# A gated mix of an S5 scan and an H3 convolution: the first time block's two pairs of B.x are turned by ScalarE, and halves, gates and scalings change places

## The chip, the core and the metric

The kernel runs on one core of one Trainium2 chip. The core has TensorE (PE, matmuls), VectorE (DVE), ScalarE (ACT), GpSimd (POOL) and SyncE (SP); each takes its own instructions in order, and they wait for one another by semaphores. DMAs are issued here from SyncE's queue (plain and transposing loads, stores) and from GpSimd's (gathers that add to what lies at their destination); a few small loads come from ScalarE's. The metric is the time of one execution on the device, in microseconds, as the median of several runs. The profile's trace is that of a single execution.

## The reference, cut to what matters

Inputs are bf16; x is [1, 2048, 1024] (time by channel), and the state has P = 1024 complex components.

```python
def _A_ref(x, Lambda_re, Lambda_im, B_re, B_im, C_re, C_im, log_dt, Dskip):
    Lam_bar = jnp.exp(jnp.exp(log_dt) * Lam)
    B_bar = ((Lam_bar - 1.0) / Lam)[:, None] * Bmat
    Bu = jnp.einsum("bld,pd->blp", x + 0j, B_bar)
    for t in range(L):
        h = Lam_bar[None, :] * h + Bu[:, t, :]
    y = 2.0 * jnp.einsum("blp,dp->bld", hseq, Cmat).real + x * Dskip
def _B_ref(q, k, v, shift_k, ssm_k, ssm_D):
    kv = k_shift * v            # k_shift: 4 taps of k along time
    y = irfft(rfft(kv_pad) * rfft(kf_pad))[:S] + kv * ssm_D
    return q * y
g = sigmoid((x * gate_w).sum(-1, keepdims=True))
out = g * _A_ref(x, ...) + (1 - g) * _B_ref(x, B_k, B_v, ...)
```

## The kernel before, in words

**Two halves.** The H3 part (the long convolution `_B_ref`) goes channel tile by channel tile, eight tiles of 128 channels; its results go to a scratch tensor in DRAM (`cv_scr`). The S5 part (`_A_ref`) goes by time blocks of 512 steps (`tb` 0 to 3) and by groups of 256 state components (`g` 0 to 3). It starts as filler between the H3 rounds and then has the rest of the kernel.

**A round of the H3 part** is one pass of the loop `for c in range(NC - 1)` (L1132), c = 0 to 6; the eighth channel's products follow behind the loop. Round c does the products in frequency of channel c on VectorE (`products`, L664), the transform of the next channel n = c + 1 on TensorE (`fwd_K`, `fwd_V`, into PSUM tiles `psk` and `psv`, which ScalarE evicts to Kh and Vh), the inverse transform of channel c - 1 (`inverse`, L716, PSUM tile `psz`, evicted to `cv` and stored), and the taps of channel c + 2 (`taps`, L562). `times_v` (L592) multiplies the tap sums `ks` by v on VectorE and then mirrors them on TensorE. The first product of a channel, `G<-Kh,Vh` (or `G<-BT,Vh`, where an even channel's spectrum of K lies in a tile named BT), reads the whole of Vh. A second part of G is added by a gather from GpSimd (`G<-wkh`).

**B.x** is computed for 16 blocks (`order`, L766): the list index i runs over (tb, g) = (0,0), (0,1), (1,0), (1,1), (2,0) and so on. A block has two tiles (j = 0, 1) of 128 components. The time steps of a block are kept as evens (a = 0) and odds (a = 1), 256 each, since the scan runs over pairs of steps: an even step's entry is turned into even + lam times the odd step before it. x is loaded transposed, in two halves: half h of time block tb holds the steps of parity h (`load_xT`, L250), and a = h reads it. Block 1's half 1 is loaded in round 2 and its half 0 in round 3, at L1228:

```python
            if nn + 1 < NC:
                load("kT", nn + 1, True)
                load("kn", nn + 1)
                apart = spread(nn + 1)
                step(apart)
...
                elif c in (2, 3):
                    load_xT(1, (3 - c,))
```

`load(..., True)` writes a column with ScalarE first (`hold`), so that the load waits for ScalarE's place in the order. `spread` copies kT to kB on SyncE's queue.

**The lam-multiples** are made in two ways. Blocks i = 0 and 1 (time block 0) use `Bu_tile` (L813): TensorE multiplies the odd steps by diagonal matrices of lam (`lamd`, made by `lam_diag`, L770: four times 128x128 products with the identity and two with -lam's for each group, by ScalarE in round 0 and by VectorE in round 1) and adds them in PSUM. All other blocks use `turn_U` (L872): six ScalarE passes write lam times the odd steps to a tile Q, in two parts, and after each part a gather from GpSimd adds Q to the evens. Blocks 2 and 3 are computed by `Bu_halves` (L838), odds first, then evens, each 16 matmuls of 256 columns; from block 4 on by `Bu_plain` (512 columns).

**The order.** Every engine's instructions stand in the order of the program (`put`, L92). The tiles of blocks 0 to 3 are one generator, `parts` (L1129), and each `step(parts)` in a round takes it to its next `yield`. A tile of `Bu_tile` has three steps (odds, evens, lam matmuls), and a tile of `Bu_halves` also has three (odds, evens, nothing). The 24 calls: round 1 four (before the taps, after `times_v`, two between the halves of `fwd_V`), round 2 five, round 3 four, round 4 five, round 5 four, round 6 two.

**After the rounds.** `gate(tb)` (L748) are 32 matmuls of one column and two small sigmoids. C's eight tiles (`turn_C`, L1274) are scaled too: m = the other part times a factor (ScalarE), the tile times its factor (ScalarE for tiles 0 and 1, VectorE for the others), and then the sum, for tiles 0, 1, 4, 5 by gathers. Tiles 4 and 5 keep m in the four buffers of the pool Q, where `turn_U` of the later blocks gets its Q as well. The 16 scans (`scan`, L891) then run on VectorE, each with 256-long scans, rotations, and lam-multiples q of the result hb, by VectorE or, for the scans in `scaled_by_act`, by ScalarE. TensorE multiplies by C (`Cy`, `Cy_group`, PSUM tile `psy`). Filler steps that a loop puts on the list `on_act` are taken between B.x tiles (`Bu_next`, L1365). `stamp` (L1169) is a small GpSimd copy at the start of round 6 that waits for x of time block 2.

Of the kernel before, what the change touches and what calls it, by code (L numbers as in the profile page):

```python
# [20 lines left out]
def kernel(  # L21
# [64 lines left out]
    def ps2(shape, name):  # L86
        return psum.tile(shape, F32, name=name, tag="ps")
# [29 lines left out]
    def act(o, i, **kw):  # L117
        put("act", nc.scalar.activation, out=o, in_=i, **kw)
# [648 lines left out]
    order += [(NTB - 1, g) for g in range(NG)]  # L767
    ends = consts.tile([128, 2, NG, 2, 2], BF16, name="ends")

    def lam_diag(g, home, on_act=False):  # L770

        if g == 0:
            lamd["all"] = home.tile([128, 2, 2, 3, 128], BF16, name="lamd", tag="lamd")
        t = lamd[g] = lamd["all"][:, g]
        for j in range(2):
            for k, f in enumerate((lam[:, 0], lam[:, 1], mlam)):
                pi = 2 * g + j
                if on_act:
                    act(t[:, j, k], ident, func=ACT.Identity, scale=f[:, pi:pi + 1])
                else:  # L780
                    ts(t[:, j, k], ident, f[:, pi:pi + 1], None, ALU.mult)

    def Bu(i):
        tb, g = order[i]
        if i == 13:
            V_ = s5p["v13"].tile([128, 2, 2, HB], BF16, name="V13")
            O_ = lam_pool.tile([128, 2, 2, HB + 2], BF16, name="O13", tag="lamd")
            Us[tb, g] = V_, O_[:, :, :, 2:]
            turns_U[i] = turn_U(g, V_, O_)
            return [Bu_plain(tb, g, V_, O_, j) for j in range(2)]  # L790
        if i in (10, 11):
            if i == 10:
                s5p["u2"] = xt_pool.tile([128, 2, 2 * (4 * HB + 4)], BF16, name="U2", tag="xT")
            U = s5p["u2"][:, i - 10]
        else:
            shape = [128, 2 * (4 * HB + 4)]
            if i in (6, 7, 8, 15):
                U = u4(shape, BF16, "U")
            else:
                home = uu[0 if i in (0, 1, 14) else 1] if i < 6 or i == 14 else s5p["uu"]  # L800
                U = home.tile(shape, BF16, name="U")
        if i >= 2:
            V_, O_ = U[:, 0:4 * HB], U[:, 4 * HB:]
            V_ = V_.rearrange("p (c j t) -> p c j t", c=2, j=2)
            O_ = O_.rearrange("p (c j t) -> p c j t", c=2, j=2)
            Us[tb, g] = V_, O_[:, :, :, 2:]
            turns_U[i] = turn_U(g, V_, O_)
            return [(Bu_halves if i < 4 else Bu_plain)(tb, g, V_, O_, j) for j in range(2)]
        U = U[:, 0:8 * HB].rearrange("p (a c j t) -> p a c j t", a=2, c=2, j=2)
        Us[tb, g] = U[:, 0], U[:, 1]  # L810
        return [Bu_tile(tb, g, U, j) for j in range(2)]

    def Bu_tile(tb, g, U, j):  # L813
        xT = xTs[tb]
        ps = []
        d = lamd[g][:, j]
        for a in (1, 0):
            ps.append(ps2([128, 2, HB], ("even", "odd")[a]))
            for c in range(2):
                for dt_ in range(ND):  # L820
                    mm(ps[1 - a][:, c], BT[g][:, c, dt_, j * 128:(j + 1) * 128], xT[:, dt_, a * HB:(a + 1) * HB],
                       dt_ == 0 and (a == 1 or c == 0), a == 1 and dt_ == ND - 1)
            if a == 1:
                act(U[:, 1, :, j], ps[0], func=ACT.Copy)
                if j == 1 and tb < NTB - 1:
                    act(ends[:, tb % 2, g], U[:, 1, :, :, HB - 1], func=ACT.Copy)
                yield
        yield
        for k, c, o in ((0, 0, 0), (0, 1, 1), (1, 0, 1), (2, 1, 0)):
            if tb > 0:  # L830
                mm(ps[1][:, o, 0:1], d[:, k], ends[:, 1 - tb % 2, g, c, j:j + 1], False, False)
            mm(ps[1][:, o, 1:HB], d[:, k], U[:, 1, c, j, 0:HB - 1], False, k == 2)
        act(U[:, 0, :, j], ps[1], func=ACT.Copy)
        yield

    turns_U = {}

    def Bu_halves(tb, g, V_, O_, j):  # L838
        if j == 0:
            act(O_[:, :, :, 1], ends[:, 1 - tb % 2, g], func=ACT.Copy)  # L840
        for a in (1, 0):
            ps = ps2([128, 2, HB], ("even", "odd")[a])
            for c in range(2):
                for dt_ in range(ND):
                    mm(ps[:, c], BT[g][:, c, dt_, j * 128:(j + 1) * 128], xTs[tb][:, dt_, a * HB:(a + 1) * HB],
                       dt_ == 0, dt_ == ND - 1)
# [7 lines left out]
        yield  # L854

    def Bu_plain(tb, g, V_, O_, j):
        xT = xTs[tb]
        if j == 0 and tb > 0:
            act(O_[:, :, :, 1], ends[:, 1 - tb % 2, g], func=ACT.Copy)
        elif j == 0:  # L860
            act(O_[:, :, :, 1], lam[:, :, 0:2], func=ACT.Copy, scale=0.0)
        ps = ps2([128, 2, 2, HB], "both")
        for c in range(2):
            for dt_ in range(ND):
                mm(flat(ps[:, c]), BT[g][:, c, dt_, j * 128:(j + 1) * 128], xT[:, dt_], dt_ == 0, dt_ == ND - 1)
        act(O_[:, :, j, 2:], ps[:, :, 1], func=ACT.Copy)
        if j == 1 and tb < NTB - 1:
            act(ends[:, tb % 2, g], O_[:, :, :, HB + 1], func=ACT.Copy)
        act(V_[:, :, j], ps[:, :, 0], func=ACT.Copy)
        yield  # L870

    def turn_U(g, V_, O_):  # L872
        both = slice(0, 2)
        for part in (((both, both, lam[:, 0]),), ((0, 1, lam[:, 1]), (1, 0, mlam))):
            if s5p["Q"] is s5p["wu"]:
                if part[0][0] == both:
                    whole_Q = u4([128, 2, 2, 2, HB], BF16, "Q")
                Q = whole_Q[:, part[0][0] != both]
            else:
                Q = s5p["Q"].tile([128, 2, 2, HB], BF16, name="Q")  # L880
            for j in range(2):
                pi = 2 * g + j
                for c, o, f in part:
                    act(Q[:, o, j], O_[:, c, j, 1:1 + HB], func=ACT.Identity, scale=f[:, pi:pi + 1])
            gather(V_, Q)
            yield

    put_off = []
    scaled_by_act = (4, 12, 13, 14)

    def scan(tb, g, fin):  # L891

# [6 lines left out]
        for js in ([slice(0, 1), slice(1, 2)] if last else [slice(0, 2)]):  # L899
# [39 lines left out]
            if tb * NG + g == 3:  # L939
                run(turning[7])  # L940
                product(0)
            if by_act and tb == NTB - 1:
                q = [s5p["Q"].tile([128, 2, 2, HB], BF16, name="Q") for k in range(2)]
            else:
                q = [w2([128, 2, 2, HB], BF16, "q") for k in range(2)]
# [119 lines left out]
    def step(gen):  # L1065
        next(gen, None)
# [65 lines left out]
    for c in range(NC - 1):  # L1132
        n, nn = c + 1, c + 2
        if c == 0:
# [28 lines left out]
            step(apart)  # L1163
            load_xT(0, (1,))
            run(apart)
            lam_diag(0, lam_pool, True)
            continue
        if c == 6:
            put("pool", nc.gpsimd.tensor_copy, stamp, xTs[2][:, 0, 0:HB + 1:HB])  # L1169
# [1 line left out]
        step(old)  # L1171
        step(tabs)
        if c == 6:
            step(parts)
        step(back)
        step(tv)
        steps(prod, 3)
# [11 lines left out]
        if c == 2:  # L1189
            step(parts)  # L1190
        fwd_K(n, (0, 1))
        if c in (2, 6):
            step(parts)
        fwd_K(n, (2, 3))
        if c == 4:
            step(parts)
# [6 lines left out]
        if nn < NC:  # L1203
# [2 lines left out]
            step(fk)  # L1206
            if c < 5:
                step(fk)
            if c == 4:
                step(parts)  # L1210
            if c == 1:
                load_BT(1, 0, True)
            elif c < 5:
# [35 lines left out]
            run(next(tiles))  # L1249
            run(next(tiles))  # L1250
        fwd_V(n, (0, 1))
        if c < 6 and c != 4:
            step(parts)
            if c in (1, 3):
                step(parts)
        fwd_V(n, (2, 3))
        if c in (4, 5):
            step(parts)
        if c == 1:
            lam_diag(1, lam_pool)  # L1260
        old = tabs

    h3r.close()
# [10 lines left out]
    def turn_C(pi):  # L1274
# [7 lines left out]
            act(m[c], CT[pi][:, 1 - c], func=ACT.Identity, scale=mc2i[:, pi:pi + 1])  # L1282
            yield
        for c, f in enumerate((c2r, mc2r)):
            if pi < 2:
                act(CT[pi][:, c], CT[pi][:, c], func=ACT.Identity, scale=f[:, pi:pi + 1])
            else:
                ts(CT[pi][:, c], CT[pi][:, c], f[:, pi:pi + 1], None, ALU.mult)
            if by_sum:
                gather(CT[pi][:, c], m[c])  # L1290
        if not by_sum:
            tt(CT[pi], CT[pi], whole_m, ALU.add)

# [4 lines left out]
    with tc.tile_pool(name="fin", bufs=1, side="right") as fin:  # L1298
# [6 lines left out]
        prod, back = products(c, 0, room, False), inverse(c - 1)  # L1305
        run(old)
        steps(prod, 3)
        run(turns_U[3])
        run(next(tiles))
        steps(turning[0], 2)  # L1310
        step(back)
        steps(turning[1], 2)
        run(back)
        gate(1)
        gate(2)
        steps(prod, 2)
        b6, b7 = Bu(6)
        run(b6)
        run(b7)
        run(turns_U[6])  # L1320
        run(turning[0])
# [111 lines left out]
    for j in range(NS):  # L1433
# [6 lines left out]
        advance(j)  # L1440
        for t in turning[2 * j:2 * j + 2]:
            run(t)
        on_act += [lambda t=t: step(t) for t in turning[2 * j + 2:2 * j + 4] for _ in range(2)]
        turn = turns_U[turned[j]] if j in turned else none
        if j != 10 and plan[j][0:1] != "G":
            step(turn)
# [82 lines left out]
```

## Time and profile before

| what | value |
| --- | --- |
| median of 3 runs | 384.33 us (384.24 to 385.03) |
| the profiled execution | 384.57 us, span of its instructions 382.8 us |
| granted TensorE clock, mean | 0.998 |
| ScalarE's passes of one turn (171.20 to 174.0 us) | 2.85 us |
| matmul of 512 / 256 columns, start to start | 0.216 / 0.11 us |
| DMA | 71.77 MB, mean 187 GB/s |
| gather U<-Q, 256 KB, issue to landing, median | 5.3 us |
| gather G<-wkh, 768 KB, issue to landing, median | 8.8 us |

How to read it: times within the trace are microseconds from the first instruction of the program. The listing by groups gives out<-in by the program's names, so `even<-U,lamd` is a matmul that writes the PSUM tile "even" from U and lamd; nearly all instructions stand at L94, the helper that issues them, so tiles tell more than lines. A timeline row is start, duration, engine, line, operation, out<-in, shape and count, and in brackets how long the engine was idle before it and what ended that. Matmuls overlap in the pipeline, so the distance between starts tells more of their rate than their duration does.

### The profile page before, as it was taken

The page shows a single profiled execution, that of the slowest core. Times are in us where ns is not written, and L with a number is a line of the kernel's source. Part 1 is how long each engine was busy: PE and PEld are TensorE (multiplying, and loading weights), DVE is VectorE, ACT ScalarE, POOL GpSimd, SP SyncE. Part 2 cuts the span into 40 slices and gives each one's busy share as a digit, 9 for nine tenths or more (in the row PEclk, how much of TensorE's full clock was granted, in tenths as well). Part 3 has the DMA queues.
Part 4 walks back from the last instruction along what each step waited for, and adds up shares of the span by engine and source line. Part 5 has one row for each costly group of instructions (what it writes and reads, how often), then busy time and mean ns, then how long its engine had stood idle before and what let it go on. Part 6 is the DMA issues. An engine that isn't in the chain of part 4 may idle for free.

```text
span 382.8 us, 6633 instructions
## 1 busy us (share of the span) xinstructions
PE 371.3 (97%) x2419; PEld 198.3 (52%) x2453; DVE 371.2 (97%) x599; ACT 303.6 (79%) x469; POOL 81.8 (21%) x108
## 2 busy tenths in 40 slices
PE   7899999999999999999999999989999999999995
PEld 5566458575584846744454444434444444444442
DVE  7999999999999999999999999999999999999996
ACT  5898998988979999786979699675989759937601
POOL 4011030020301102031003110413414323634100
PEclk9999999999999999999999999999999999999999
DMA  7979999998999997959999999986899999898903
GB/s 166 165 108 223 218 205 205 245 203 211 201 164 211 208 213 169 198 125 154 192 221 164 226 203 250 213 153 125 150 222 192 208 245 246 136 250 156 238 8 110
DMA packets 126402, 71.77 MB, mean 187 GB/s; under 512 B 104665, under 2 KB 107489, under 8 KB 126370
## 3 DMA queue, kind: packets, MB, share of 16 engines
q1 hardware_dynamic: 111232, 45.64, 55.4%
q0 software_dynamic: 12976, 25.17, 38.9%
q10 hardware_dynamic: 2162, 0.54, 0.8%
q8 instruction: 19, 0.31, 0.3%
q14 instruction: 13, 0.11, 0.1%
HBM read 15.48 MB, written 8.39 MB: 62 GB/s over the span
## 4 chain that ended last, share of the span: by engine, by line
PE 52%; DVE 30%; issue 9%; DMA 4%; ACT 3%; ACTq 1%; POOL 0%; DVEq 0%; POOLq 0%
PE psy L94 29%; PE both L94 15%; DVE BT L94 11%; DVE wkh L94 8%; DVE G L94 5%; DVE t L94 3%; PE psz L94 2%; DVE ks L94 2%; PE psk L94 2%; DMA CT<-Q 2%; DMA pbb<-cv_scr 1%; PE psv L94 1%; DMA rows<-in_gate_w_dram 1%; PE p L94 1%; PE taps L94 1%
## 5 line engine op out<-in xcount | busy, mean ns | idle before, releaser
L94 PEld LDWEIGHTS <-BT 128*128 128x128 bf16 x640 | 62.0, 98 | 48.3 <-issue 0.2
L94 PE MATMUL both<-xT,BT 128*128 128x512 bf16 x375 | 83.0, 379 | 0.4
L94 POOL DMA_DIRECT2D U<-Q x26 | 26.7, 1039 | 88.8 <-ACT Q L94 31.0
L94 PEld LDWEIGHTS <-hb 128*128 128x128 bf16 x256 | 24.9, 98 | 31.4 <-issue 1.6
L94 PEld LDWEIGHTS <-U 128*128 128x128 bf16 x240 | 23.5, 98 | 28.3
L94 PE MATMUL psy<-CT,hb 128*128 128x512 bf16 x157 | 36.3, 379 | 0.1
L94 ACT ACTIVATE Vh<-psv 128x1024 bf16<-128x1024 f32 x32 | 30.7, 1034 | 5.3 <-PE psv L94 5.3
L94 PE MATMUL psy<-CT,U 128*128 128x512 bf16 x149 | 34.6, 379 | 0.2
L94 ACT ACTIVATE Q<-U,lam 128x512 bf16<-128x512 bf16 (+1 forms) x52 | 29.9, 612 | 4.9 <-DMA CT<-Q 4.9
L94 DVE TENSOR_TENSOR_SCAN W<-rv,init,A 128x256 bf16<-128x256 f32 x48 | 32.2, 730 | 0.0
L94 POOL DMA_DIRECT2D G<-wkh x8 | 9.7, 1218 | 102.8 <-DVE wkh L94 102.8
L94 ACT ACTIVATE U<-both 128x512 bf16<-128x512 f32 x44 | 24.1, 595 | 8.0 <-PE both L94 7.5
L94 PEld LDWEIGHTS <-SF 128*128 128x128 bf16 x184 | 18.0, 98 | 19.7 <-issue 1.4
L94 PE MATMUL psk<-eok,SF 128*128 128x512 bf16 (+1 forms) x119 | 27.9, 354 | 0.3
L94 PE MATMUL psz<-G,CI 128*128 128x512 bf16 x64 | 24.3, 379 | 0.1
L94 PE MATMUL psz<-G,SI 128*128 128x512 bf16 x64 | 24.3, 379 | 0.0
L94 PE MATMUL psy<-CTa,hb 128*128 128x512 bf16 x94 | 22.6, 379 | 1.2 <-ACT U L94 1.0
L94 PE MATMUL taps<-dg,kT 128*128 128x128 bf16 (+1 forms) x352 | 21.7, 210 | 0.8 <-DMA kT<-in_B_k_dram 0.8
L94 PEld LDWEIGHTS <-kT 128*128 128x128 bf16 x352 | 21.0, 100 | 2.5 <-DMA kT<-in_B_k_dram 2.1
L94 DVE TENSOR_TENSOR wkh<-BT,Vh 128x3072 bf16<-128x3072 bf16 (+4 forms) x20 | 21.8, 1110 | 0.0
L94 DVE TENSOR_TENSOR wkh<-Kh,Vh 128x3072 bf16<-128x3072 bf16 (+2 forms) x16 | 21.2, 1348 | 0.0
L94 PE MATMUL psy<-CTa,U 128*128 128x512 bf16 x87 | 20.4, 379 | 0.1
(227 smaller groups left out, 846.1 us busy)
## 6 DMA issues: line engine op xcount, KB each, us to landing
U<-Q POOLq DMA_DIRECT2D x26, 256.0 KB, 5.3
G<-wkh POOLq DMA_DIRECT2D x6, 768.0 KB, 8.8
cv_scr<-cv SPq DMA_DIRECT2D x16, 256.0 KB, 5.7
kn<-in_B_ssm_k_dram SPq DMA_DIRECT2D x5, 512.0 KB, 4.0
v<-in_B_v_dram SPq DMA_DIRECT2D x5, 512.0 KB, 6.2
out_dram<-m SPq DMA_DIRECT2D x8, 256.0 KB, 4.5
BT<-cv_scr SPq DMA_DIRECT2D x7, 256.0 KB, 5.9
out_dram<-BT SPq DMA_DIRECT2D x7, 256.0 KB, 2.0
```

The source lines that it names most:

```text
L94: i = f(*a, **kw)
```

## The change

Blocks 0 and 1 are computed by `Bu_halves` too and turned by ScalarE and gathers; `Bu_tile` and `lam_diag` go. A tile now has two steps, so 16 calls of `step(parts)` are left: three in round 1, four in round 2, three each in rounds 3, 4 and 5, none in round 6. The turn of block 0 stands at the start of round 6, that of block 1 where block 3's stood, and block 3's turn goes behind the first tile of block 6; where `s5p["Q"]` is None, their Q lies in the table NCF and in the room of `lamd`. Gates 1 and 2 move ahead of the inverse transform of channel 6. C's tiles 4 and 5 are scaled by ScalarE, with their gathers inside the filler steps. Scan 11's lam-multiples go to ScalarE, with q in the pool Q.

```diff
-    def lam_diag(g, home, on_act=False):
...
     def Bu(i):
...
-        if i >= 2:
-            V_, O_ = U[:, 0:4 * HB], U[:, 4 * HB:]
...
-        return [Bu_tile(tb, g, U, j) for j in range(2)]
-
-    def Bu_tile(tb, g, U, j):
...
+        V_, O_ = U[:, 0:4 * HB], U[:, 4 * HB:]
+        V_ = V_.rearrange("p (c j t) -> p c j t", c=2, j=2)
+        O_ = O_.rearrange("p (c j t) -> p c j t", c=2, j=2)
+        Us[tb, g] = V_, O_[:, :, :, 2:]
+        turns_U[i] = turn_U(g, V_, O_)
+        return [(Bu_halves if i < 4 else Bu_plain)(tb, g, V_, O_, j) for j in range(2)]
     def Bu_halves(tb, g, V_, O_, j):
         if j == 0:
-            act(O_[:, :, :, 1], ends[:, 1 - tb % 2, g], func=ACT.Copy)
+            before(tb, g, O_)
...
             yield
-        yield
+
+    def before(tb, g, O_):
+        if tb > 0:
+            act(O_[:, :, :, 1], ends[:, 1 - tb % 2, g], func=ACT.Copy)
+        else:
+            act(O_[:, :, :, 1], lam[:, :, 0:2], func=ACT.Copy, scale=0.0)
...
+            elif s5p["Q"] is None and part[0][0] == both:
+                Q = NCF.rearrange("p o (j t) -> p o j t", j=2)
+            elif s5p["Q"] is None:
+                Q = lam_pool.tile([128, 2, 2, HB], BF16, name="Qb", tag="lamd")
...
-    scaled_by_act = (4, 12, 13, 14)
+    scaled_by_act = (4, 11, 12, 13, 14)
...
-            if by_act and tb == NTB - 1:
+            if by_act and tb > 1:
...
-            lam_diag(0, lam_pool, True)
...
         if c == 6:
-            step(parts)
+            s5p["Q"] = None
+            run(turns_U[0])
...
         fwd_K(n, (0, 1))
-        if c in (2, 6):
-            step(parts)
         fwd_K(n, (2, 3))
...
-            if c == 4:
-                step(parts)
...
         fwd_V(n, (0, 1))
-        if c < 6 and c != 4:
+        if c < 4:
             step(parts)
-            if c in (1, 3):
-                step(parts)
         fwd_V(n, (2, 3))
-        if c in (4, 5):
+        if c == 5:
             step(parts)
-        if c == 1:
-            lam_diag(1, lam_pool)
...
-            if pi < 2:
+            if by_sum:
                 act(CT[pi][:, c], CT[pi][:, c], func=ACT.Identity, scale=f[:, pi:pi + 1])
             else:
                 ts(CT[pi][:, c], CT[pi][:, c], f[:, pi:pi + 1], None, ALU.mult)
             if by_sum:
                 gather(CT[pi][:, c], m[c])
+                yield
...
-        run(turns_U[3])
+        run(turns_U[1])
         run(next(tiles))
+        gate(1)
+        gate(2)
         steps(turning[0], 2)
         step(back)
         steps(turning[1], 2)
         run(back)
-        gate(1)
-        gate(2)
         steps(prod, 2)
         b6, b7 = Bu(6)
         run(b6)
+        s5p["Q"] = None
+        run(turns_U[3])
+        s5p["Q"] = s5p["wu"]
         run(b7)
...
-        on_act += [lambda t=t: step(t) for t in turning[2 * j + 2:2 * j + 4] for _ in range(2)]
+        if j > 0:
+            on_act += [lambda t=t: step(t) for t in turning[2 * j + 2:2 * j + 4] for _ in range(4 if j == 1 else 2)]
```

More of the change, by code (lines that the diff above doesn't have):

```diff
@@ L768 @@
     ends = consts.tile([128, 2, NG, 2, 2], BF16, name="ends")
-    def lam_diag(g, home, on_act=False):
[L772 to L781, printed above, removed]
     def Bu(i):
@@ L801, in Bu @@
                 U = home.tile(shape, BF16, name="U")
-        if i >= 2:
-            V_, O_ = U[:, 0:4 * HB], U[:, 4 * HB:]
[L804 to L810, printed above, removed]
-        return [Bu_tile(tb, g, U, j) for j in range(2)]
-    def Bu_tile(tb, g, U, j):
[L814 to L826, printed above, removed]
-                yield
[L828 to L834, printed above, removed]
+        V_, O_ = U[:, 0:4 * HB], U[:, 4 * HB:]
[4 more added lines that the diff above has]
+        return [(Bu_halves if i < 4 else Bu_plain)(tb, g, V_, O_, j) for j in range(2)]
     turns_U = {}
@@ L853, in Bu_halves @@
             yield
-        yield
+    def before(tb, g, O_):
[3 more added lines that the diff above has]
+            act(O_[:, :, :, 1], lam[:, :, 0:2], func=ACT.Copy, scale=0.0)
     def Bu_plain(tb, g, V_, O_, j):
         xT = xTs[tb]
[L858 to L861, printed above, removed]
+        if j == 0:
+            before(tb, g, O_)
         ps = ps2([128, 2, 2, HB], "both")
```

## The prediction

> **What bounds the kernel now.** I read the page's busy shares, then the chain of waits, then the timeline of one channel round, engine by engine.
>
> ```profile
> PE 371.3 (97%) x2419; PEld 198.3 (52%) x2453; DVE 371.2 (97%) x599; ACT 303.6 (79%) x469; POOL 81.8 (21%) x108
> ```
>
> TensorE and VectorE are both full; ScalarE has a fifth to spare. "Busy" can hide stalls, so I took the distance from start to start: 128x512 matmuls follow each other every 0.216 us and 128x256 ones every 0.11 us, with few holes. VectorE has no hole over 0.11 us between 31 and 378 us.
>
> ```profile
> 114.25 0.44 DVE G L94
> 115.39 1.22 DVE G L94
> 116.61 1.14 DVE ks L94
> ...
> 253.15 9.01 PE psy L94 x41
> ```
>
> In the chain, the channel rounds (to about 164 us) are VectorE's, and the end is TensorE's. In the rounds TensorE meets VectorE once per round, at `mirror` (it waits for `ks`), and arrives 0 to 0.5 us early. So work taken from TensorE in the rounds becomes waiting there, while work added to a round, or a wait inside it, can hold VectorE up.
>
> **Counting the halves.** I call the four blocks i = 0 to 3 with their two tiles each t0 to t7, and a half "odd" or "even". Before, every tile has three steps (odd, even, then the lam matmuls, or nothing). After, it has two. Round 1 has three step calls left (before the taps, after `times_v`, between the `fwd_V` halves), round 2 four, round 3 three. Calls 8, 9 and 10 are those of round 3, so they run t3 even, t4 odd, **t4 even**. Before, round 3 ended with t4 odd, and t4 even came after round 4's `fwd_K`. t4 is of time block 1, and its even half reads half 0 of that block's x, which round 3 itself loads (L1228, with c = 3). That load is not moved.
>
> ```profile
> 112.16 0.60 PE L94 MATMUL even<-U,lamd 128*128 128x255 bf16 x4
> 112.60 1.91 PE L94 MATMUL odd<-xT,BT 128*128 128x256 bf16 x16
> 114.34 0.59 PE L94 MATMUL psv<-ev,CF 128*128 128x512 bf16 x2
> ...
> 126.16 1.91 PE L94 MATMUL even<-xT,BT 128*128 128x256 bf16 x16
> ```
> ```profile
> 116.42 1.11 SPq L94 DMA_DIRECT2D kB<-kT  x2
> 117.58 3.23 SPq L94 DMA_TRANSPOSE xT<-in_A_x_dram  x1
> ```
>
> The first fence is TensorE in round 3: t4 even must now run at 112, between the two `psv` groups, instead of at 126. The second is SyncE's queue: the half of x is only issued at 117.58, behind `kB<-kT`, which waits for kT. The sixteen counts of its semaphore come at 124.6 to 124.8. Nothing in the change makes SyncE earlier. So TensorE stands still, and behind it in its queue are `psv` (whose eviction Vh VectorE reads next), `psz` and `mirror`.
>
> **The sum, step by step.**
>
> 1. TensorE's arrival. Round 2 loses two groups of four lam matmuls (0.44 us each) and gains one half (1.75): +0.87. The 0.53 us that TensorE waited before `mirror` at 94.79 cover part of it and 0.34 is left, so t4 even is reached at 112.16 + 0.34 = 112.5. The six `lamd` products that VectorE loses (70.66 to 71.64, 0.98 us) gain nothing here:
>
> ```profile
> 92.00 1.96 ACT L94 ACTIVATE Vh<-psv 128x1024 bf16<-128x1024 f32 x2
> 94.65 2.28 DVE L94 TENSOR_TENSOR G<-Kh,Vh 128x4096 bf16<-128x4096 bf16 x1
> ```
>    That product needs the last Vh, which ended at 93.96; behind 0.87 us more of matmuls it ends near 94.6, where VectorE began before.
>
> 2. The landing. From issue to landing 7.1 us in this trace. The two halves of time block 2 took 7.2 (154.80 to 162.0) and 5.1 us. SyncE comes 0.34 later, since the ScalarE pass that releases kT follows this round's taps, and the 768 KB gather that shared the queues from 121.91 is not there yet. I take 124.5; bounds 123.0 and 125.1.
>
> 3. Restart. Then come t4 even (1.75) and what lay between 114.34 and the last Vh's end (117.35): 3.01 us.
>
> 4. The clock. TensorE has then been idle for 12 us. The trace shows both what a pause does and what a restart costs:
>
> ```profile
> 4.53:5.03 0.50, 0.50 (x5) 0.00 (x0) 0.00 (x0) 1.00 1.44 166
> 6.03:6.53 0.50, 0.50 (x13) 0.00 (x0) 0.00 (x0) 1.00 1.26 221
> ```
> ```profile
> 378.00:383.00 5.00, 0.58 (x3) 0.08 (x1) 1.61 (x3) 0.00 (x0) 0.00 (x0) 0.80 0.41 150
> ```
>    The first two rows are the first tap matmuls in windows of half a microsecond (busy time, then the count of matmuls), the third is the end, for all engines (the last three columns are granted clock, DMA share and GB/s). At the start the same matmuls go at half pace (5 against 13), from the first matmul at 1.19 until about 5.5: 4.3 us. At the end the granted clock is 0.80 over 5 us: half speed from 2.4 us after the last matmul on. So I charge 4.3 us at half pace, 2.15 us lost; bounds 0 (the clock stays up) and 4.3 (it opens twice as late). The Trainium skill's page "TensorE: Matmul & The Clock Gate" (Part 1) says that one idle window of about 3.4 us halves the clock, and one busy window of a free-running grid restores it. By that, 3.4 to 6.8 us would go at half pace and 1.7 to 3.4 be lost; the trace's 4.3 us lies inside.
>
> 5. VectorE reads Vh at 124.5 + 1.75 + 3.01 + 2.15 = 131.4 instead of 117.66: **+13.7 us**. After that, rounds 4 to 6 have as much or less matmul work than VectorE work (round 4: TensorE 22.7, VectorE 23.0), so nothing grows, and nothing is won back: VectorE has no hole to close.
>
> **The rest of the change.**
>
> - The 16 lam matmuls (16 x 0.11 = 1.75 us of TensorE) lie in VectorE's rounds, and so does the half taken from round 6 (1.75): worth 0.
> - Block 0's two turns in round 6: six ScalarE passes each (171.20 to 174.0: 2.85 us), in the 2.6 us of holes around 160 to 164 and in place of an eviction: 0. Their gathers lie behind the stamp on GpSimd:
>
> ```profile
> 165.20 1.29 POOL L94 COPY stamp<-xT 128x2 bf16<-128x2 bf16 x1 [11.94 <-ACT cv L94]
> 168.41 1.20 POOL L94 DMA_DIRECT2D G<-wkh  x1 [1.92 <-DVE wkh L94]
> 172.86 0.86 POOL L94 DMA_DIRECT2D U<-Q  x1 [0.74 <-ACT Q L94]
> 178.09 0.86 POOL L94 DMA_DIRECT2D U<-Q  x1 [4.38 <-DMA U<-Q]
> ```
>    The second gather of a pair waits until the first has landed (172.86 to 177.5). Put ahead of `G<-wkh`, the pair delays it by about 3.7 us; it landed at 174.9 and VectorE reads it at 181.1, so 6.2 us cover that and the shared queues. I charge 0; if the cover is gone, 1 to 2 us.
> - Gates 1 and 2 ahead of `psz` fill the 0.18 us that TensorE waited at 188.0: -0.18. Block 1's turn goes into a ScalarE hole of 2.4 us (198.0 to 200.4): 0, at most 0.5 later for one eviction that has a spare buffer.
> - Tiles 5 and 6 of C:
>
> ```profile
> ACT Q L94 <- DMA CT<-Q: 4.9, 1, 4.9
> PE psy L94 <- ACT U L94: 1.0, 1, 1.0
> ```
>    ScalarE waited 4.9 us for a Q buffer, because VectorE's scaling (four of 0.40 us at 244) let the gathers go late; TensorE then lost 1.2 us at 252 waiting for an eviction. Now ScalarE scales (4 x 1.04 = 4.2 us), the buffers are free by 240, and laying its queue out again from 221 on gives the eviction's end at 251.8, when TensorE comes: -1.17. Bounds 0 and -1.2.
> - Scan 11's lam-multiples: VectorE loses 4 x 0.26, ScalarE gains 4 x 0.62 where it is 74% busy. TensorE sets the end there without a hole: 0, bounds -0.3 and +0.3.
>
> Sum against the profiled execution: 384.57 + 13.7 - 0.18 - 1.17 = 396.9. That execution lies 0.24 above the median of the runs shown, so 396.7 beside 384.33.
>
> **The rivals.**
>
> - *The half of x is there in time* (the other side). It decides by its landing: up to 112.9 VectorE would not notice, and every microsecond later costs one. Then only the late gains stand: 384.33 - 1.35 = 383.0, faster. For it: SyncE is idle from 101.6 to 107.4 and could issue earlier. Against: its order is fixed, and v, kT and kB stand ahead. 7%.
> - *The wait comes, the clock stays up*: step 4 falls out, 394.5. For it: the trace has no pause inside the program; against: the last row of step 4. 10%.
> - *The pair of gathers delays G beyond its cover* as well: VectorE waits 1 to 2 us at 181, 398.2. For it: the listing of waits has one of 7.3 us for such a landing; against: 6.2 us of cover. 18%.
>
> The forecast itself: 65%. A difference of under 0.2%, 0.8 us, can't be told from none. Faster 6%, same 2%, slower 92%. The range, 393.8 to 399.4, takes in the first step's bounds and the last two rivals.
>
> **What would show it.** In the changed kernel's trace: a hole of about 12 us in TensorE near 112, ended by the transfer of x; granted clock below 1 behind it; VectorE idle for about 13 us before `G<-BT,Vh`; no wait of 4.9 us of ScalarE on `CT<-Q`; `G<-wkh` of round 6 behind two `U<-Q`. No hole at 112 would make the forecast wrong at once; a hole with full clock makes it 2 us too high.

## The result and the profile after

The changed kernel takes 405.32 us (median of 6 runs, 403.97 to 409.42), the kernel before 384.73 beside it: ratio 1.0553, 95% interval 1.05 to 1.0606. That is slower, as forecast, but 8.6 us above the forecast of 396.7 and outside its range. Some executions took some per cent longer than the others of the same kernel, and one of the kernel before took 2227 us; the ratios leave these out, so a median can lie above its ratio.

The profiled execution took 405.34 us. Busy time of the engines on its page, then TensorE's clock in the 40 slices of the span:

```profile
PE 373.8 (93%) x2403; PEld 198.2 (49%) x2437; DVE 367.9 (91%) x585; ACT 314.7 (78%) x485; POOL 84.5 (21%) x112
...
PEclk9999999999975999999999999999999999999999
```

TensorE and VectorE stood still for 11 to 12 us of the span each before; now it is 30 and 36 us. The first hole is where the forecast put it. TensorE's timeline in round 3, VectorE's, and SyncE's queue:

```profile
112.43 0.59 PE L94 MATMUL psv<-ks,SF 128*128 128x512 bf16 x2
123.47 3.60 PE L94 MATMUL even<-xT,BT 128*128 128x256 bf16 x16 [10.44 <-DMA xT<-in_A_x_dram]
126.86 1.06 PE L94 MATMUL psv<-ev,CF 128*128 128x512 bf16 x2
```
```profile
94.88 2.29 DVE L94 TENSOR_TENSOR G<-Kh,Vh 128x4096 bf16<-128x4096 bf16 x1 [1.21 <-ACT Vh L94]
...
131.00 2.29 DVE L94 TENSOR_TENSOR G<-BT,Vh 128x4096 bf16<-128x4096 bf16 x1 [13.02 <-ACT Vh L94]
```
```profile
115.69 1.11 SPq L94 DMA_DIRECT2D kB<-kT  x2
116.85 3.46 SPq L94 DMA_TRANSPOSE xT<-in_A_x_dram  x1
```

t4 even waits for x, which SyncE issues at 116.85, and VectorE waits 13.02 us for the Vh behind it: 131.00 instead of 117.66. The row at 94.88 shows that the 0.98 us of `lamd` products are lost in a wait for Vh. Windows of TensorE (busy time and count, then the granted clock, DMA share, GB/s): while it waits, while it restarts, and after.

```profile
115.00:123.40 8.40, 0.00 (x0) 0.53 1.04 218
123.40:129.20 5.80, 5.73 (x22) 0.50 0.04 9
129.20:131.00 1.80, 1.80 (x9) 1.00 0.00 0
```

To see where the rest comes from I took the start of the same instruction in both traces and the difference. This table is the backbone of what follows (us later than in the kernel before):

| point (its time in the kernel before) | after |
| --- | --- |
| VectorE reads the Vh of round 4 (117.7) | 13.34 |
| TensorE: first tile of block 4, in round 6 (170.7) | 13.35 |
| TensorE: tile at 197.1 | 13.16 |
| TensorE: tile at 218.3 | 17.00 |
| TensorE: first row of y (253.2) | 17.65 |
| VectorE: scan 11 (329.0) | 13.60 |
| VectorE: scan 13 (346.9) | 21.22 |
| the last instruction | 20.68 |

So there are three steps: 13.35 us in round 3, **4.3 us on TensorE between round 6 and the first row of y** (17.65 - 13.35; below, the middle), where -1.35 was forecast, and **7.6 us on VectorE between scans 11 and 13**, where 0 was forecast. The listing of waits for the second step (TensorE, then ScalarE) and the third (VectorE):

```profile
PE both L94 <- DMA BT<-in_A_B_re_dram: 2.8, 1, 2.8
...
PE psy L94 <- ACT U L94: 1.7, 1, 1.7
PE both L94 <- ACT U L94: 0.5, 1, 0.5
```
```profile
ACT U L94 <- DMA U<-Q: 6.0, 1, 6.0
```
```profile
DVE U L94 <- ACT Q L94: 8.7, 2, 7.0
```

ScalarE's wait of 4.9 us on `CT<-Q` is gone, as forecast, but TensorE's wait ahead of the first row of y is 1.7 instead of 1.0. GpSimd's queue shows the added gathers:

```profile
179.79 0.85 POOL L94 DMA_DIRECT2D U<-NCF  x1
185.41 0.86 POOL L94 DMA_DIRECT2D U<-Qb  x1 [4.78 <-ACT Kh L94]
185.95 1.55 POOL L94 DMA_DIRECT2D G<-wkh  x1
...
215.12 0.86 POOL L94 DMA_DIRECT2D U<-NCF  x1 [6.72 <-ACT NCF L94]
220.08 0.86 POOL L94 DMA_DIRECT2D U<-Qb  x1 [4.11 <-issue]
220.62 1.20 POOL L94 DMA_DIRECT2D U<-Q  x1
227.23 0.86 POOL L94 DMA_DIRECT2D U<-Q  x1 [5.40 <-ACT U L94]
```

Block 0's pair stands ahead of `G<-wkh`, block 3's ahead of block 6's, whose second gather is issued at 227.23; a later block's U takes the buffer that it reads, and ScalarE waits for that until 233.03.

### The profile page after: what moved, and what is told of

Same layout as the page of the kernel before. It is cut to its first block, busy times and chain, and to the rows that moved or that the text cites. A ratio compares the mean times of both kernels' runs of the same rounds, so it can differ in the third digit from the quotient of the medians.

```text
span 403.5 us, 6610 instructions
## 1 busy us (share of the span) xinstructions
PE 373.8 (93%) x2403; PEld 198.2 (49%) x2437; DVE 367.9 (91%) x585; ACT 314.7 (78%) x485; POOL 84.5 (21%) x112
## 5 line engine op out<-in xcount | busy, mean ns | idle before, releaser
L94 POOL DMA_DIRECT2D U<-Q x26 | 28.3, 1088 | 73.9 <-DMA U<-Q 28.8
L94 PE MATMUL even<-xT,BT 128*128 128x256 bf16 x128 | 17.0, 291 | 10.4 <-DMA xT<-in_A_x_dram 10.4
L94 PE MATMUL psv<-ks,SF 128*128 128x512 bf16 x64 | 19.5, 387 | 2.5 <-DMA ks<-lo 2.2
```

The source lines that it names most:

```text
L94: i = f(*a, **kw)
```

## The experiments

**The half of x: alone, and taken out.** In the kernel before, t4 even alone is moved to round 3:

```diff
         fwd_K(n, (2, 3))
-        if c == 4:
-            step(parts)
...
             if c in (1, 3):
                 step(parts)
+            if c == 3:
+                step(parts)
```

> The kernel before, with nothing changed but t4's even half taken in round 3 (a third step between the two halves of the transform of v) instead of in round 4. Theory A: this alone brings the hole: 384.7 + 13.3 = 398.0. Rival B: the hole needs the change's other moves as well (in the kernel before, TensorE reaches this place 0.3 us earlier and round 4 has the lam matmuls still, but rounds 4 to 6 then have slack of TensorE to win back): 390 to 396.

Measured: 398.25 us (397.79 to 399.32), ratio 1.0341 (1.028 to 1.0401). VectorE's row:

```profile
130.93 2.29 DVE L94 TENSOR_TENSOR G<-BT,Vh 128x4096 bf16<-128x4096 bf16 x1 [13.13 <-ACT Vh L94]
```

It comes 13.27 us later, and the last instruction 13.20: one moved half, nothing won back. Theory A holds. The other way round, the changed kernel with the half loaded a round earlier:

```diff
-                elif c in (2, 3):
-                    load_xT(1, (3 - c,))
+                elif c == 2:
+                    load_xT(1, (1,))
                 run(apart)
+                if c == 2:
+                    load_xT(1, (0,))
```

> The kernel after, with half 0 of time block 1's x loaded at the end of round 2, behind the last copy to kB, instead of in round 3. Theory A (three separate costs: 13.3 us for the wait for this half and what follows it, 4.3 us between round 6 and the first row of y, 3.0 us in the last scans): the hole at 112.6 goes, the clock stays up, VectorE reads the last Vh again near 117.7, and nothing else moves: 405.3 - 13.3 = 392.0. Rival B: the hole is only the first of several things that are late in rounds 3 to 6 (the other loads of round 3 move with it), so the next of them takes a part of it back: 394 to 400, with a new wait of VectorE in rounds 3 to 6.

Ratio 1.0191 (1.0116 to 1.0266); the median of its four runs is 396.88 us (392.56 to 402.51), and the profiled one took 393.14. The hole is gone: VectorE reads the Vh of round 4 1.75 us later than in the kernel before, and 1.7 us of this are there at 20 us already. Counted from there the last instruction is 6.8 us late, 14.0 less than in the changed kernel: theory A, by the trace. TensorE does not stop:

```profile
114.01 0.59 PE L94 MATMUL psv<-ks,SF 128*128 128x512 bf16 x2
114.44 1.91 PE L94 MATMUL even<-xT,BT 128*128 128x256 bf16 x16
```

**The clock's share of it.** In the changed kernel, 46 matmuls of constants fill the hole:

```diff
             ps = ps2([128, 2, HB], ("even", "odd")[a])
+            if (tb, g, j, a) == (1, 0, 0, 0):
+                for _ in range(46):
+                    mm(flat(ps), ident, CF[:, 0], True, True)
```

> The kernel after, with 46 more 512-column matmuls of constants into the same PSUM tile ahead of t4's even half, so that TensorE works through the hole; they are overwritten and change no result. They take 46 x 0.216 = 9.9 us and end before x lands at 123.4. Theory A: the granted clock stays at 1 behind the hole, the 5.7 us at half pace go, VectorE reads Vh 2.9 us earlier: 405.3 - 2.9 = 402.4. Rival B: the half pace behind the hole is not the clock's but the pace of waiting (x landing piece by piece), or it is covered by VectorE's own work: 405.3, no change. Rival C: the matmuls end late and hold t4's even half up: above 405.3.

Measured 404.0 us (401.91 to 406.23), ratio 1.0481 (1.0416 to 1.0546). In the profiled execution, the slowest of the four, x landed at 125.5, 2 us later than in the changed kernel, so a hole of 2.45 us was left, and the clock still fell. The windows are that stretch (with the end of the last constant matmul), the restart, and after:

```profile
122.90:125.50 2.60, 0.17 (x1) 1.00 0.74 168
125.50:129.20 3.70, 3.68 (x18) 0.54 0.02 2
129.20:131.00 1.80, 1.80 (x10) 1.00 0.00 0
```

From the landing to VectorE's read it is 6.5 us here and 7.6 us in the changed kernel, so the shorter half pace is worth 1.1 us. The three other runs have a mean clock of 0.995 to 0.997, where the changed kernel has 0.97 to 0.98, so there it was at half for 4 us at most (0.005 of the span, doubled), the end of the kernel included: 401.91, 403.78 and 404.23 us. That speaks for theory A, but the spread is as large as the 2.9 us, so their size is read from the changed kernel's trace alone.

**One step of B.x in round 6 instead of round 2.** So t4 even lies in round 4 again, with the load of x where it is:

```diff
         if c == 6:
+            step(parts)
             s5p["Q"] = None
...
-        if c == 2:
-            step(parts)
         fwd_K(n, (0, 1))
```

> The kernel after, with one of round 2's four steps of B.x taken out and one put into round 6, so that t4's even half comes in round 4 again; the load of x stays where it is. Theory A: the 13.35 us go, and since round 2 now has three halves (5.25 us of matmuls) where the kernel before had 6.1, the 0.98 us that VectorE no longer spends on lamd show up as well: 405.3 - 13.35 - 1.0 = 391.0. Rival B: only the hole goes, the last Vh of round 3 still holds VectorE: 392.0. Rival C: the half that is now in round 6 delays cv and the loads of C behind it, and the wait for BT's last part grows: 393 to 396.

393.45 us (390.91 to 394.26), ratio 1.0218 (1.0189 to 1.0247). In the trace the hole goes, and VectorE keeps 0.97 us of `lamd` (0.54 us ahead at 20 us, 1.51 ahead from round 3 to round 6). But the waits for BT grow to 5.2 us:

```profile
PE both L94 <- DMA BT<-in_A_B_re_dram: 2.9, 1, 2.9
PE both L94 <- DMA BT<-in_A_B_im_dram: 2.3, 1, 2.3
PE psy L94 <- ACT U L94: 1.7, 1, 1.7
```

Theory A's gain in the rounds is right; rival C names what took it back.

**Scan 11.** In the kernel before, only scan 11's lam-multiples go to ScalarE; in the changed kernel, only they go back (the reverse of the first line):

```diff
-    scaled_by_act = (4, 12, 13, 14)
+    scaled_by_act = (4, 11, 12, 13, 14)
...
-            if by_act and tb == NTB - 1:
+            if by_act and tb > 1:
```

> The kernel before, with scan 11's lam-multiples on ScalarE with q in the pool Q as in the change, and nothing else. Theory A: this alone brings the waits for Q's buffers and for q: 384.7 + 3.0 = 387.7. Rival B: in the kernel before, the gathers of the last turns come earlier, the buffers are free in time, and it costs nothing: 384.7 +- 0.4.

> The kernel after, with scan 11's lam-multiples on VectorE again, as before. Theory A: the 3.0 us at the end come from this, since q of scan 11 now waits in the four buffers of the pool Q for the gathers of the last turns and VectorE's sums wait for q (8.7 us in two waits): 402.3. Rival B: the end is late because the turns of the last blocks are late from the middle on, whoever multiplies: 405.3 +- 0.5.

Alone it costs more than I thought: 390.54 us (389.17 to 395.65), ratio 1.0116 (1.008 to 1.0151). Taken back, the changed kernel falls to 402.21 (401.0 to 405.54), ratio 1.0405 (1.0318 to 1.0492). ScalarE's and VectorE's timelines of the kernel before with this edit alone:

```profile
335.74 0.49 ACT L94 ACTIVATE Q<-U,mlam 128x256 bf16<-128x256 bf16 x1
338.81 1.33 ACT L94 ACTIVATE Q<-hb,lam 128x512 bf16<-128x512 bf16 x2 [2.58 <-DMA U<-Q]
345.48 1.33 ACT L94 ACTIVATE Q<-hb,lam 128x512 bf16<-128x512 bf16 x2 [5.33 <-DMA U<-Q]
```
```profile
340.18 0.69 DVE L94 TENSOR_TENSOR U<-U,Q 128x1024 bf16<-128x1024 bf16 x1 [0.53 <-ACT Q L94]
346.84 0.76 DVE L94 TENSOR_TENSOR U<-U,Q 128x512 bf16<-128x512 bf16 x2 [5.97 <-ACT Q L94]
```

q now lies in the pool Q, whose four buffers hold the turns of the last blocks. A buffer comes free when the gather that reads it has landed, so ScalarE waits 2.58 and 5.33 us, and VectorE waits 6.5 us for q where it had no hole at all. Theory A has the cause right and the size too small. The edit moves the multiples to ScalarE and q to the pool Q together; no run gave ScalarE another room for q, so that the room alone is at fault rests on these two waits.

**The middle: gathers, order, or ScalarE's load.** Five kernels, all made from the changed one. First, block 0's turn at the end of round 6 instead of its start:

```diff
-        if c == 6:
-            s5p["Q"] = None
-            run(turns_U[0])
...
         if c == 5:
             step(parts)
+        if c == 6:
+            s5p["Q"] = None
+            run(turns_U[0])
+            s5p["Q"] = s5p["wu"]
```

> The kernel after, with the turn of block 0 (six ScalarE passes and two gathers) at the end of round 6 instead of at its start. Theory A: the two gathers no longer stand ahead of the gathers for G and ks, cv is stored 2 us earlier, C's and B's transposes are issued earlier, and the 3.0 us that TensorE waits for BT's last part at 213 go: 402.3 to 403. Rival B: this wait comes from the store of C's loads behind ScalarE's hold and from the shared queues, not from the order of gathers: 405.3 +- 0.5. Rival C: the turn at the end of the round pushes block 1's and block 3's gathers further back, and ScalarE's wait for U's buffer grows beyond 6.0 us: 406 to 408.

406.34 us (404.43 to 407.63), ratio 1.0537 (1.0478 to 1.0596): no gain. In the trace the loss of the middle grows from 4.3 to 8.5 us (11.29 us later in round 6, 19.75 at the first row of y). Measured from round 6, the first load of BT's last part was issued 3.2 us earlier than in the changed kernel, but the second landed 1.3 us later: three gathers, issued at 198.9 to 203.9 and landed up to 210.9, ran beside them. Rival C: ScalarE's wait for U's buffer grew from 6.0 to 9.2 us, and the queues did the rest. Next, C's third tile is loaded behind BT's last part:

```diff
-                load_CT(pi)
+                if pi < 2:
+                    load_CT(pi)
...
     load_BT(3, 1)
+    load_CT(2)
     load_CT(3)
```

> The kernel after, with the load of C's third tile taken behind the two loads of BT's last part on SyncE's queue, so that these start about 2.8 us earlier. Theory A: the 3.0 us that TensorE waits for BT's last part go, the rest of the middle (0.6 and 0.65 us) and the end stay: 402.3. Rival B: the transfers of these loads share the queues with the two added pairs of gathers, and land as late as before: 405.3 +- 0.7. Rival C: SyncE then waits for BT's room, which VectorE's products of channel 6 hold, and everything behind comes later: above 405.3.

405.51 us (404.75 to 408.21), ratio 1.0556 (1.0526 to 1.0585). TensorE's waits from 178 to 300 us, all of them:

```profile
PE both L94 <- ACT U L94: 3.2, 1, 3.2
```

The wait for BT is gone, and the one for the eviction grew from 0.5 to 3.2: the wait moved on to the next thing that was late, block 6's second gather. So that one was moved as well, by taking block 3's turn behind C's first two tiles (together with the edit above):

```diff
-        s5p["Q"] = None
-        run(turns_U[3])
-        s5p["Q"] = s5p["wu"]
         run(b7)
...
         run(turning[1])
+        s5p["Q"] = None
+        run(turns_U[3])
+        s5p["Q"] = s5p["wu"]
```

> The kernel after, with C's third tile loaded behind BT's last part and block 3's turn taken behind the turns of C's first two tiles; nothing left out. Theory A (the waits are of order): BT lands in time and the second gather of block 6 comes before U8's buffer is wanted, so neither wait is left: 401 to 401.5. Rival B (the added transfers are late for something wherever they stand): another wait of 2 to 4 us comes up, on a turned tile of C or on block 3: 403.5 to 405.5.

404.29 us (403.3 to 406.72), ratio 1.0489 (1.0438 to 1.054). TensorE's waits in the same stretch:

```profile
PE psy L94 <- ACT U L94: 2.8, 1, 2.8
PE both L94 <- ACT U L94: 1.8, 1, 1.8
...
```

Both old waits are gone (12.24 us later at 197.1 and at 218.3), and evictions by ScalarE are late instead (15.98 at the first row of y). That is rival B, at another place than it named. What changed is ScalarE's load: windows of its busy time in the last third of the middle, of the kernel before and of the changed one, show it busy for 22.87 of 28.15 us and for 28.58 of 28.80.

```profile
225.00:253.15 28.15, 22.87 (x37) 1.00 1.06 221
```
```profile
242.00:270.80 28.80, 28.58 (x43) 1.00 1.12 227
```

In the ordered kernel itself this stretch lasts 31.93 us; ScalarE is busy for 28.38 of them and waits 3.3 us for a buffer of the pool Q that a gather still reads. Its load leaves no room for that wait. (The 28.8 us of the next expectation are the changed kernel's.) So C's scaling was taken off it again, in this ordered kernel:

```diff
-            if by_sum:
+            if pi < 2:
                 act(CT[pi][:, c], CT[pi][:, c], func=ACT.Identity, scale=f[:, pi:pi + 1])
...
                 gather(CT[pi][:, c], m[c])
-                yield
...
-        if j > 0:
-            on_act += [lambda t=t: step(t) for t in turning[2 * j + 2:2 * j + 4] for _ in range(4 if j == 1 else 2)]
+        on_act += [lambda t=t: step(t) for t in turning[2 * j + 2:2 * j + 4] for _ in range(2)]
```

> The ordered kernel (after, with C's third tile loaded behind BT's last part and block 3's turn behind the turns of C's first two tiles), with C's tiles 5 and 6 scaled by VectorE as before. Theory A (with both waits gone by order, what is left is ScalarE's load: 28.4 us busy of the 28.8 that TensorE's matmuls need there): 4.2 us less of ScalarE take the 3.7 us away, so the first row of y comes 12.0 to 13.2 us later than in the kernel before, and the time falls from 404.3 to 400 to 401.5. Rival B (the place of block 3's turn, between the evictions, is what is late): 403 to 405.

404.12 us (401.63 to 404.72), ratio 1.0466 (1.0417 to 1.0516). TensorE's first row of y is 13.75 us later, and round 6 was 13.91 later: the middle costs nothing any more, as theory A says, though ScalarE still waits there, 2.7 and 2.1 us: it has the room now. But the time hardly fell, where theory A forecast 400 to 401.5. VectorE still waits for q, by the listing of its waits, and the last instruction is 19.90 later:

```profile
DVE U L94 <- ACT Q L94: 7.2, 1, 7.2
```

That overturned my sum of three costs: the middle's and scan 11's **lie beside each other**, one on TensorE's path and one on VectorE's. Last, the gathers of blocks 0 and 1 are left out of the changed kernel and ScalarE's passes kept (B.x then lacks the lam-multiples of these blocks):

```diff
-        turns_U[i] = turn_U(g, V_, O_)
+        turns_U[i] = turn_U(g, V_, O_, i > 1)
...
-    def turn_U(g, V_, O_):
+    def turn_U(g, V_, O_, summed=True):
...
-            gather(V_, Q)
+            if summed:
+                gather(V_, Q)
```

> The kernel after, with the gathers of blocks 0 and 1 left out and ScalarE's passes for them kept (so the lam-multiples of these two blocks are missing from B.x). Theory A (the middle's 4.3 us are these four gathers, 1 MB: they delay BT's last part in the shared queues and the gathers behind them in GpSimd's order): both waits go, the first row of y begins as far behind the kernel before as round 6 ends, 13.35 us, or 1.2 less for C's scaling: 405.3 - 4.3 = 401.0, down to 399.8. Rival B (ScalarE's twelve passes, and C's scaling on ScalarE, are what is late): at least half of the 4.3 us stay: 403 to 405.

402.83 us (401.85 to 404.19), ratio 1.0445 (1.0398 to 1.0491), between the two forecasts. The wait for BT goes, the eviction's wait (1.4) and that ahead of y (1.7) stay; the middle costs 2.1 us (14.03 to 16.13). So about half of it is the added gathers; the rest, by the two runs before, is ScalarE's load and the place of block 3's turn.

**C's scaling by itself.** The edit taken back in the changed kernel, and alone in the kernel before (the reverse of the last diff but one), there also with the gates' new place:

> The kernel after, with C's tiles 5 and 6 (counted from 1) scaled as before: their own factors by VectorE, the steps and gathers in the order of before. Theory A: ScalarE gets 4.2 us of its load between 233 and 276 back, but VectorE scales late again and the 4.9 us wait for a Q buffer comes back; TensorE's wait ahead of the first row of y stays at 1.2 to 1.9 us: 405.3 +- 0.7. Rival B: the 4.3 us in the middle are the scaling on ScalarE, which is busy without a hole there: 401 to 403. Rival C: the scaling is worth what was predicted, and taking it back costs 1.2 us: 406.5.

> The kernel before, with C's tiles 5 and 6 scaled by ScalarE as in the change, and nothing else. Theory A: the 4.9 us wait for a Q buffer goes, the first row of y begins 0 to 1.2 us earlier: 383.5 to 384.7. Rival B: the 4.2 us more of ScalarE hold the evictions of the B.x tiles 9 to 12 up: 385.5 to 388.

> The kernel before with C's tiles 5 and 6 scaled by ScalarE and gates 1 and 2 ahead of the inverse transform of channel 6, and nothing else. Theory A: the gains that the prediction gave them hold here, where ScalarE has the room: 384.7 - 1.2 - 0.2 = 383.3. Rival B: no gain that can be measured: 384.3 to 385.

Ratios 1.0411 (1.0317 to 1.0506), 0.9964 (0.9922 to 1.0007) and 1.0003 (0.9971 to 1.0035). In the second trace TensorE's wait ahead of y is gone and its lateness falls by 1.14 us, the forecast's 1.17; in the third it is 1.7 us again, and ScalarE's waits have the long one of the changed kernel:

```profile
ACT U L94 <- DMA U<-Q: 6.2, 1, 6.2
```

A gain of about 1 us is there in one trace, and the times of the two kernels do not confirm it. In the changed kernel the scaling costs rather than gains: taking it back brings the first row of y from 17.65 - 17.00 = 0.65 us of loss to 15.61 - 16.81 = -1.2.

**All at once.** The half a round earlier, scan 11 back, C's third tile and block 3's turn later; then also C's scaling back on VectorE. A third kernel is the one before with the parts that looked like gains: C's scaling, the gates' place, and the second `lamd` made by ScalarE (`lam_diag(1, lam_pool, True)`).

> The kernel after with the half of x loaded in round 2, scan 11 on VectorE, C's third tile loaded behind BT's last part, and block 3's turn behind the turns of C's first two tiles. Theory A: all three costs go and the gains of C's scaling and the gates are left: 384.7 - 1.2 - 0.2 = 383.3. Rival B: the wait of the middle stays in some form: 386 to 389.

> As e15_all (half of x early, scan 11 on VectorE, C's third tile behind BT's last part, block 3's turn later), with C's tiles 5 and 6 scaled by VectorE as before. Theory A: nothing of the loss is left, and of the gains only the gates' 0.2: 384.5 to 386. Rival B: 389 to 391, as with C's scaling on ScalarE.

> The kernel before with only what was found to gain: C's tiles 5 and 6 scaled by ScalarE, gates 1 and 2 ahead of the inverse transform of channel 6, and the second group's lamd made by ScalarE instead of VectorE. The lam matmuls stay on TensorE, scan 11 on VectorE. Theory A: 384.7 - 1.2 - 0.2 - 0.5 (of the 0.98 us that VectorE saves, about half, since TensorE's wait ahead of the mirror of round 3 was 0.53) = 382.8. Rival B: ScalarE's six more passes in round 1 delay an eviction there and the last two gains are lost in waits: 383.5 to 384.7.

Ratios 1.018 (1.0109 to 1.0251), **1.0022 (0.9983 to 1.0062)** and 1.001 (0.9974 to 1.0047). The first lies above both of its forecasts: in its trace the middle still costs 4.15 us (1.23 late in round 6, 5.38 at the first row of y), in the second's nothing (8.35 and 8.22). With every cause undone the loss is gone by the ratio: theory A of the second. But the median of the second's ten runs is 389.73 us (384.64 to 395.74); its trace is of an execution of 392.87 us, in which TensorE waits 6.2 us in round 3 for the gather `ks<-lo`, and why half of its executions are longer stays open. Nothing is measurably faster than the kernel before, and the third missed theory A's 382.8. A variant of the first with the step of B.x in round 6 and x left alone came to 1.0128 (1.011 to 1.0146), above both of its forecasts:

> The kernel after with four things mended at once: the step of B.x moved from round 2 to round 6, scan 11's lam-multiples back on VectorE, C's third tile loaded behind BT's last part, and block 3's turn behind the turns of C's first two tiles, so that its gathers no longer stand ahead of those of block 6. Theory A (the three costs are separate and all of them are of order, not of work): 384.7 - 1.0 (lamd) - 1.2 (C's wait) - 0.2 (gates) = 382.3, faster than both kernels. Rival B (the two more pairs of gathers cost something wherever they stand): 384.5 to 388.

Which waits were left in it stays open: its trace is of an execution of 394.34 us, where the median is 389.8.

## Why the prediction was wrong, step by step

The same table for the kernels that decide it, us later than before:

| point | after | x early | scan 11 back | ordered | ordered, C back | before + half moved | before + scan 11 |
| --- | --- | --- | --- | --- | --- | --- | --- |
| Vh of round 4 | 13.34 | 1.75 | 12.27 | 12.04 | 13.90 | 13.27 | -0.26 |
| first row of y (TensorE) | 17.65 | 6.09 | 16.39 | 15.98 | 13.75 | 13.20 | -0.13 |
| scan 11 (VectorE) | 13.60 | 2.02 | 12.32 | 11.92 | 14.00 | 13.26 | -0.26 |
| scan 13 (VectorE) | 21.22 | 9.09 | 12.31 | 19.35 | 20.12 | 13.26 | 5.14 |
| last instruction | 20.68 | 8.53 | 16.38 | 18.80 | 19.90 | 13.20 | 5.27 |

Read the columns downward. With scan 11 back the end is TensorE's first row of y (16.39, 16.38). With the middle mended the end is VectorE's (20.12, 19.90). The end follows the later of the two.

- **Steps 1 to 5 were right**: +13.35 against +13.7, and 13.27 when done alone. The `lamd` gain is lost as said. x landed at 123.4, not 124.5: SyncE issued it at 116.85, 0.7 us earlier than before and not 0.34 later, and it took 6.6 us, not 7.1. Half pace lasted 5.7 us, not 4.3: t4 even took 3.39 instead of 1.75 us and the four pairs of `psv` 2.89 instead of 1.73, so 2.8 us were lost, not 2.15. These two errors, 1.1 us too late and 0.65 too little, cancel in part, so that the sum is off by only 0.35 us is partly luck. Two small readings were off as well: the counts of 5 against 13 overstate the half pace (those matmuls follow each other every 0.106 and 0.056 us), and SyncE was idle from 100.3, not 101.6.
- **Gates, -0.18**: right; TensorE's lateness falls from 13.35 to 13.16 there.
- **Block 0's pair ahead of G, 0**: right for VectorE (13.35 us late in round 5, 13.37 at 189 us, no wait), so the third rival did not come; G's gather landed at 193.1, which took 4.9 of the 6.2 us of cover. But only G was followed. The added gathers delayed BT's last part, which had landed just in time (without them it does so again), and block 3's pair in its new place delayed block 6's second gather. This is what the step missed; I had looked at the queue's next reader, not at those behind it.
- **Tiles 5 and 6 of C, -1.17**: failed; that stretch lost 0.65 us instead. It laid ScalarE's queue out from 221 on as if nothing else came later. But ScalarE had waited 6.0 us for block 6's gather, and with what this pushed back and the scaling it is full (28.58 of 28.80 us).
- **Scan 11's lam-multiples, 0 with bounds of 0.3: this is the step that failed.** It measured 7.6 us on VectorE's path inside the change, and 5.4 when done alone; that, more than any other term, puts the time above the range. It weighed busy shares ("74% busy") and TensorE's end. It did not ask where q is written and what frees that room, nor that VectorE, which this profile showed without a hole up to 378 us, passes on any wait.

The sum as it came out: 384.57 + 13.35 (half of x) + 0.25 (to scan 11) + 7.6 (scan 11) - 0.55 (won back behind it) = 405.2, beside the profiled 405.34. The middle's 4.3 us is not in it; it shows where scan 11 is on VectorE (16.38 - 12.27 = 4.1 us in that trace). So the middle is a second failed step: with scan 11 back the time is still 402.2 us, with the middle mended 404.1, both above the range. Why ScalarE waits 6.2 us for block 6's gather in the kernel before with C's scaling and the gates' new place, and 2.2 with the scaling alone, stays open; no run moved the gates alone.

## What to carry to other kernels

When work goes to an engine with time to spare, ask first which buffer it writes, what frees that buffer, and who waits for the result: a busy share answers none of these. When transfers are added, follow everything behind them in the queue up to the last one that had landed just in time. Take the lateness at fixed points of each engine and let the later path set the end: costs on two paths do not add, and mending one of them shows next to nothing.

## What was not expected of the hardware

How long a hole is does not alone tell whether TensorE's clock falls. In the changed kernel the wait for x brought it to half from 115.55 us, 2.5 us after the last matmul, to 129.20. In the kernel with constant matmuls a hole of 2.45 us was enough, and it was at half from 125.73 to 129.15. But the wait for BT in the changed kernel, 2.84 us from 213.47 to 216.31, left it at full speed. The traces show why: every change of the clock in all 20 of them stands a whole number of steps of 3.41 us from the other changes of its trace. In such steps, TensorE of the changed kernel (busy time and count, then the granted clock, DMA share, GB/s):

```profile
112.14:115.55 3.41, 0.89 (x5) 1.00 1.22 178
115.55:129.20 13.65, 5.73 (x22) 0.50 0.59 130
...
214.53:217.95 3.42, 1.64 (x8) 1.00 1.25 240
217.95:221.36 3.41, 3.32 (x16) 1.00 1.50 223
```

The step ahead of the fall was idle for 2.52 us. The wait for BT is cut by the end of a step at 214.53, and neither part has more than 1.8 us. In the 20 traces every step at full clock with 2.00 us or more of idle time was followed by half clock (the least in the kernel with C's third tile later, 367.03 to 370.44), and none with 1.94 or less. This is read off from the traces; no run varied a hole to test it.

The Trainium skill's page "TensorE: Matmul & The Clock Gate" (Part 1) puts the drop after an idle window of about 3.4 us. The length agrees, but a step that was idle in part was enough here, and the measurement decides. One to two of its windows, an estimate of 3.4 to 6.8 us for the way back, fit both restarts (5.7 and 3.4 us).
